# Seven block products for the first share of four more batches, and attention placed beside the other four

## The chip, the cores and the metric

One core of a Trainium2 chip runs the whole kernel. The metric is the device time of one execution in microseconds, the median of several runs. The five engines of the core that appear below are TensorE (PE, with its weight loads shown apart as PEld), VectorE (DVE), ScalarE (ACT), GpSimd (POOL) and SyncE (SP), whose queue issues all the DMAs of this kernel.

## The reference

Eight batches of eight heads, 512 local and 32 global positions, head size 64. Windowed attention feeds a gated feed-forward layer:

```python
k_all = np.concatenate([k_g, k_l], axis=2); v_all = ...
out_g = sm(scale * q_g @ k_all.T) @ v_all            # 32 global rows see everything
mask  = |i - j| <= 32                                # local rows: a band, and the 32 global keys
out_l = sm(concat([scale * q_l @ k_g.T, where(mask, scale * q_l @ k_l.T, -1e9)])) @ v_all
x = concat([out_g, out_l]).transpose(0, 2, 1, 3).reshape(4352, 512)
h = x @ w_in                                         # first product, w_in 512 x 2048
g = h * erf(softplus(h))
out = g @ w_out                                      # second product, w_out 2048 x 512
```

The inputs and weights are float32 and float64 respectively when they arrive; every large product is made of three float32r matmuls (high by high, high by low, low by high).

## The kernel before

**Two shares.** The 2048 hidden columns are 8 units of 256. Units 0 to 2 (`FIRSTU = 3`) are the first share, units 3 to 7 the second (`NQ = 5`). For each batch the first share computes h for 6 blocks of 128 columns, gates them (`gate`), multiplies them with their rows of w_out (`project`) and stores the sum to DRAM (`part`). The second share does the same for its units, loads the stored partial sum and adds it on the way out. The weights of the first share stay in SBUF (`W["in", 0, u]`). Those of the second share are split into parts early, kept in DRAM (`keep_in`, `keep_unit`) and read back later (`sums`, `fetch_unit`). The 32 global rows of all batches together make a ninth, smaller chunk, `c == B`.

**Two ways to do the first product.** In the first share, `unit` does it plainly: 4 blocks of the inner dimension by 3 matmuls, 12 matmuls of 128x512 for 128 columns of one batch. In the second share, `products` does it for two batches (`c = 2 * pr + j`) and one unit of 256 columns at once: a 2x2 by 2x2 block product by seven block multiplications instead of eight. Each of the seven (`product`) is 6 matmuls of 128x512, so a unit and a pair of batches take 42 matmuls where the plain way takes 48. For that, `pair_blocks` loads the pair's x, forms four sums on DVE and splits seven blocks into high and low; `keep_in` forms the sums on the side of the weights (`A11`, `A12`, `S1`, `A22`, `S2`, `S3`, `S4`); and the results are put together by two copies out of PSUM (`move`) and five additions on DVE (`fold`). The plain way has four copies out of PSUM for the same columns.

**Attention.** `attention` does a head: scores on PE, a masked maximum on DVE, a subtraction, the exponential on ACT, transposes on PE, the values on PE, and the normalisation mostly on DVE. The results go to DRAM (`xsc`, `xsg`) and are read back as x. The SBUF of attention is given to a second pool (`wb_pool`) once the last head is done (`ATTN`); the blocks that `pair_blocks` makes, the weight sums that `sums` loads, and part of the second share's w_out live there.

**What sets the order.** All work is entered as operations with a key, a list of engines that could do it, and an estimated duration. A planner (`Program.schedule`) walks through simulated time and gives each free engine the ready operation with the lowest key, so the instruction order on each engine is fixed when the kernel is built. Operations that may go to DVE or ACT go to whichever the planner expects free. POOL is offered to an operation that DVE can do only while the key lies under `SHARED[1]`. Keys count blocks of 128 columns of a batch: batch c of the first share has keys from 6c. Attention's heads have keys by `HKEYS`: before, head 64 lies at 33.2, so the attention is spread beside batches 0 to 5 and the PE work of the first share is mixed between its pieces.

**Order of the stages before.** Attention mixed with the first share of batches 0 to 6, then the global chunk, then batch 7 of the first share; then the second share by pairs 0 to 3; then the global chunk's second share. The lines: `keep_in` from 898, `unit` from 985, `gate` from 1021, `project` from 1074, `pair_blocks` from 1177, `products` from 1234, the loops from 1342. All matmuls are recorded at line 379, all DVE and POOL operations at 391, activations at 381, DMAs at 383.

Of the kernel before, what the change touches and what calls it, by code (L numbers as in the profile page):

```python
# [12 lines left out]
F32 = mybir.dt.float32  # L13
# [16 lines left out]
CROWD, STRETCH, EVADE = 254, 4.013, 0.302  # L30
# [5 lines left out]
HKEYS = ((0, -4.808), (11, -0.938), (22, 0.485), (64, 33.202))  # L36
STEP, GKEY = 0.082, -0.59
QLEAD, VLEAD, RLEAD, XLEAD = 0.802, -1.384, -3.274, 5.136
GOFF, POFF = 6.111, 3.439
WIN, WOUT = (1.692, -0.833, -2.539), (5.372, 5.751, 6.572)  # L40
BIASED, AG = 28, 3
SHARED = (-99.0, 10.395)
TPAIR = 3.723
KEEP, KSTEP, FIRST = 25.717, 1.786, (18.732, 17.811)
CVO = (54.239, 54.957, 78.914, 61.099, 65.318)
QLEAD2, XDEL, SLOTS = 2.849, -2.014, 11
GATE1, GATE2, PROJ1, PROJ2 = (18.529, 22.625, 24.302), (22.055, 24.328, 43.477), 16.064, 32.464
SPT = 0.35
BIAS, AHEAD = 1.579, 13.005
# [7 lines left out]
NEAR = 7.126  # L57
PAIRED, GOJOIN, GSJOIN, PTS = 16, 6, 5, 4
# [8 lines left out]
WLEAD = 2.131  # L67
LATER, GFIRST = 8, (-3.104, -5.093)
HOFF = (-0.552, -0.319, 0.052, -0.145, -0.077, -0.13, 0.035, -0.016, -0.005, -0.046, 0.01, -0.049, -0.013, 1.49, 2.105, -0.254, 0.767, 0.207, -0.21, 0.858, 0.388, -0.382, 1.584, -2.479, 0.129, -0.149, -0.895, 0.741, 3.078, -0.931, 2.609, 4.711)
XOFF = (-1.743, 3.531, 4.132, 6.479, -2.355, 1.289, 6.274, -1.424, -2.0)  # L70
UOFF = (2.693, -0.229, -0.111, -0.488, 10.393, -2.037, 0.678, -8.495, 2.152)
GFF = (-0.013, 0.75, -1.267, 1.697, -1.821, -1.427, -1.715, -1.652, -1.918)
PFF = (0.156, 0.123, 0.319, 0.471, 0.761, 2.958, 1.452, 0.32, -1.362)
KQ = (2.677, 1.804, -0.704, -0.365, 4.117, -1.317, 9.687, 0.998, 2.585, -6.754)
NORMAL = 1.125 * 2.0**-15
STRAIGHT, XLATE = True, -4.089
# [264 lines left out]
def kernel(  # L341
# [553 lines left out]
    wq = [dram.tile([P, 7, 2, 256], F32, name=f"wq{q}") for q in range(NQ)]  # L895
    WQ = {(q, m): fixed(None) for q in range(NQ) for m in range(7)}

    def keep_in(q, key):
        T = []
        for i in range(2):  # L900
            TOP = View(mbuf([P, 512], F32, f"top_l_in_{q}_{i}", ("wt", "wr")[i], 1))
            ABS = View(mbuf([P, 512], F32, f"abs_l_in_{q}_{i}", "os", 4))
            to_fp32(key + KSTEP * i, w_in[NU + q, i], f"l_in_{q}_{i}", TOP, ABS, (), 1.0)
            T.append(TOP)
# [31 lines left out]

        k = key + KSTEP
        part_of(A11, a11, k)
        part_of(A12, a12, k)
        part_of(A22, a22, k)  # L940
# [80 lines left out]
    def gate(ps, c, us, key, after=(), turn=(), line=()):  # L1021
# [13 lines left out]
        add(  # L1035
            {"ACT": 2.6 + 1.31 * (ps == 0) + 1.11 * len(us)},
# [37 lines left out]
    def project(ps, c, G, at, order, after=None):  # L1074
# [15 lines left out]
        for t in range(nt):  # L1090
            for n, rows in enumerate(order):
# [3 lines left out]
                    at(n) + 0.01 * t + (TPAIR * (t // 2) if ps == 0 else 0.0),  # L1095
# [5 lines left out]
            k = at(len(order) - 1) + 0.01 * t + (TPAIR * (t // 2) if ps == 0 else 0.0)  # L1101
# [10 lines left out]
            else:  # L1112
                load(k - NU + 2, O, part[c][P * t : P * t + P, :], 262, [PART[c, t]])
                last = c == B - 1 and t == nt - 1
# [31 lines left out]

    for u in range(NQ):
        keep_in(u, KEEP + 4 * KSTEP * u + KQ[u])
        keep_unit(u, KEEP + 4 * KSTEP * u + 2 * KSTEP + KQ[NQ + u])

# [9 lines left out]
    def sums(name, q, key, order):  # L1160

        M = {}
        for n, m in enumerate(order):
# [5 lines left out]
                [WQ[q, m], ATTN],  # L1169
# [7 lines left out]
    def pair_blocks(pr, key):  # L1177
# [3 lines left out]
        for n, (i, j) in enumerate(((0, 0), (0, 1), (1, 1), (1, 0))):  # L1181
            c = 2 * pr + j
            R[i, j] = mbuf([P, 2, SL], F32, f"rx_1_{c}_{i}", "raw", RAWS)
            src = xsc[c][2 * P * i : 2 * P * i + 2 * P, :].rearrange("(k p) t -> p k t", p=P)
            load(key + 0.05 * n, R[i, j], src, 1050, [XSC[c, p] for p in range(2 * i, 2 * i + 2)] + AFTER.get(pr, []))
        T = mbuf([P, 2, SL], F32, f"rt_{pr}", "raw", RAWS)
        blocks = {}

        def block(name, n, A, k):
            HL = [Buf(pool, [P, 2, SL], F32R, f"x{x}_{pr}_{name}", tag) for x, (pool, tag) in zip("hl", XTAG[2 * n : 2 * n + 2])]  # L1190
# [43 lines left out]
    def products(name, q, X, key):  # L1234
# [22 lines left out]
        PAIR = mbuf([P, 2, SL], F32R, f"pair_{name}", ("xh", "xl")[q % 2], 3)  # L1257
# [59 lines left out]
    def last_unit(q, X, key):  # L1317


        M = sums(f"g{q}", q, key - QLEAD2, (A11, A12, S1, A22))  # L1320
# [21 lines left out]
    s = -NV  # L1342
    for c in [*range(B - 1), B, B - 1]:
        s += NU if c == B - 1 else NV
# [4 lines left out]
        for a in range(0, n, AG):  # L1349
            G |= gate(0, c, us[a : a + AG], s + a + AG + GOFF + GFF[c])  # L1350
        key = s + AG + POFF + PFF[c]
        if c < B:
            project(0, c, G, lambda n: key + 2 * n, [[(2 * u + a, 0, 2 * u + a) for a in range(2)] for u in range(NU)])
        else:
            project(0, c, G, lambda n: key + n, [[(u, 256 * a, 2 * u + a) for a in range(2)] for u in range(NU)])
# [4 lines left out]

    s0 = 17 * NU
    turns, ACTS = (), fixed(None)
    AFTER = {}
    order = [[(v, 0, v) for v in (2 * u, 2 * u + 1)] for u in range(NQ)]
    for pr in range(B // 2):
        s = s0 + 4 * NQ * pr
        X = pair_blocks(pr, s - XDEL)
        one, two = [], []
        for q in range(NQ):
            a, b, more = products(f"{pr}_{q}", q, X, s + 4 * q)  # L1370
            one += [(2 * q, a[0], ()), (2 * q + 1, a[1], ())]
# [92 lines left out]
```

## Time and profile before

| | before |
|---|---|
| runs (3) | 904.61, 904.69, 908.22 us; median 904.69 |
| profiled execution | 904.46 us |
| its span, first to last instruction | 902.7 us |
| mean granted TensorE clock | 0.996 |
| busy share of the span | PE 98%, PEld 80%, DVE 76%, ACT 60%, POOL 1% |
| moved by DMA | 188.22 MB |

The busy share of PE counts pipelined matmuls that overlap, so a full row does not by itself say that the matmuls follow at their closest pace; the spacing of matmuls in the chain of waits says that. In the views by stage, the stages are: up to 90 us attention with little else; 90 to 388 us attention with the first share; 388 to 444 us the end of the first share; then four pairs of the second share, and from 860 us the last projections.

### The profile page before, as it was taken

What the parts mean: (1) busy time and instruction counts of PE and PEld (TensorE: products, weight loads), DVE (VectorE), ACT (ScalarE), POOL (GpSimd) and SP (SyncE); (2) the same over time, 40 slices, a digit from 0 to 9 for tenths busy, and PEclk for the clock granted to TensorE, in tenths of its full rate; (3) what the DMA queues carried; (4) which work ended last, traced back from release to release, by engine and by line L of the source; (5) the groups of instructions that cost most, each with busy time, mean ns of one, the idle gap of its engine ahead of it and who ended that gap; (6) DMA issues with size and microseconds to landing.
All of it is one profiled execution on the core that took longest, in us unless ns stands there. A gap on an engine that the chain in (4) does not pass through costs nothing.

```text
span 902.7 us, 22276 instructions
## 1 busy us (share of the span) xinstructions
PE 885.5 (98%) x8807; PEld 721.2 (80%) x8807; DVE 682.9 (76%) x1821; ACT 543.7 (60%) x912; POOL 12.1 (1%) x13
## 2 busy tenths in 40 slices
PE   8789999999999999999999999999999999999998
PEld 5567787888878888888888888888888888888886
DVE  6798999969997899987898686487736965465553
ACT  5667977736673796657645583565517571553850
POOL 0002100000000000000000000000000000000000
PEclk9899999999999999999999999999999999999999
DMA  9878886888769958377499836644366426436013
GB/s 337 305 231 286 263 266 211 242 269 278 241 217 299 318 177 292 125 273 274 168 297 369 278 95 192 225 117 129 110 171 211 150 86 195 139 108 213 19 48 117
DMA packets 110016, 188.22 MB, mean 209 GB/s; under 512 B 15576, under 2 KB 39384, under 8 KB 109912
## 3 DMA queue, kind: packets, MB, share of 16 engines
q1 hardware_dynamic: 109912, 186.79, 63.7%
q8 instruction: 70, 1.15, 0.5%
q14 instruction: 34, 0.28, 0.1%
HBM read 145.59 MB, written 41.16 MB: 207 GB/s over the span
## 4 chain that ended last, share of the span: by engine, by line
PE 89%; DMA 5%; DVE 2%; ACT 2%; issue 1%; SPq 1%; DVEq 0%; ACTq 0%
PE op L379 40%; PE h L379 13%; PE pd L379 6%; PE pc L379 6%; PE pa L379 6%; PE o L379 3%; PE pb L379 3%; PE s L379 3%; PE t L380 3%; PE h_g L379 2%; PE ga L379 1%; DMA vb<-in_vB_dram 1%; PE go L379 1%; SPq L383 1%; PE gt L380 1%
## 5 line engine op out<-in xcount | busy, mean ns | idle before, releaser
L379 PE MATMUL op<-wouth,gh 128*128 128x512 f32 x544 | 215.8, 397 | 0.0
L379 PE MATMUL op<-wouth,gl 128*128 128x512 f32 x544 | 212.1, 390 | 0.0
L379 PE MATMUL op<-woutl,gh 128*128 128x512 f32 x544 | 212.0, 390 | 0.0
L382 ACT ACT_TABLE_LOAD x108 | 138.6, 1283 | 2.6 <-PEq L1451 0.7
L379 PEld LDWEIGHTS op<-wouth,gl 128*128 128x128 f32 x544 | 102.1, 188 | 21.8
L379 PEld LDWEIGHTS op<-wouth,gh 128*128 128x128 f32 x544 | 102.2, 188 | 21.5 <-issue 0.6
L379 PEld LDWEIGHTS op<-woutl,gh 128*128 128x128 f32 x544 | 102.3, 188 | 19.5
L381 ACT ACTIVATE gh<-sp 128x512 fp32r<-128x512 f32 x65 | 40.2, 629 | 104.9 <-PE op L379 88.8
L391 DVE TENSOR_TENSOR gl<-sp,gh 128x512 fp32r<-128x512 f32 x134 | 90.4, 689 | 12.8 <-PE op L379 9.3
L379 PE MATMUL h<-xh,winh 128*128 128x512 f32 (+1 forms) x216 | 85.2, 395 | 0.0
L379 PE MATMUL h<-xh,winl 128*128 128x512 f32 (+1 forms) x216 | 81.9, 379 | 0.0
L379 PE MATMUL h<-xl,winh 128*128 128x512 f32 (+1 forms) x216 | 81.7, 378 | 0.0
L381 ACT ACTIVATE sp<-sp 128x512 f32<-128x512 f32 x136 | 75.9, 622 | 0.5
L391 DVE CUSTOM_DVE_ANT_0 sm<-s,cs 128x128 f32<-128x128 f32 x256 | 57.6, 285 | 15.4 <-PE s L379 8.3
L391 DVE CAST gh<-sp 128x512 fp32r<-128x512 f32 x71 | 29.2, 422 | 36.0 <-PE op L379 35.8
L379 PE MATMUL pd<-xh_T,wq 128*128 128x512 f32 x160 | 55.6, 389 | 0.0
L379 PE MATMUL pa<-xh_B,wq 128*128 128x512 f32 x160 | 55.6, 389 | 0.0
L379 PEld LDWEIGHTS h<-xh,winh 128*128 128x128 f32 x216 | 40.6, 188 | 9.8 <-issue 2.2
L379 PEld LDWEIGHTS h<-xh,winl 128*128 128x128 f32 x216 | 40.6, 188 | 8.0
L391 DVE TENSOR_TENSOR pair<-u,pc 128x512 f32<-128x512 f32 x40 | 27.4, 685 | 24.8 <-PE pc L379 24.5
L379 PEld LDWEIGHTS h<-xl,winh 128*128 128x128 f32 x216 | 40.7, 189 | 6.7
L379 PE MATMUL o<-vb,pt 128*32 128x65 f32 x1280 | 37.7, 221 | 7.0 <-issue 5.1
(160 smaller groups left out, 1640.3 us busy)
## 6 DMA issues: line engine op xcount, KB each, us to landing
wq<-wq SPq DMA_DIRECT2D x140, 256.0 KB, 3.0
vb<-in_vB_dram SPq DMA_DIRECT2D x64, 325.0 KB, 5.6
rx<-xsc SPq DMA_DIRECT2D x30, 512.0 KB, 5.5
va<-in_vA_dram SPq DMA_DIRECT2D x64, 195.0 KB, 5.4
k<-in_kE_dram SPq DMA_DIRECT2D x32, 384.0 KB, 5.0
wq<-part SPq DMA_DIRECT2D x35, 256.0 KB, 5.0
q<-in_qT_dram SPq DMA_DIRECT2D x32, 272.0 KB, 4.5
part<-os SPq DMA_DIRECT2D x34, 256.0 KB, 4.6
```

Source lines behind the costliest of these rows:

```text
L379: pe = lambda n, *a, **k: pinned(nc.tensor.matmul(n, *a, **k))
L380: tr = lambda *a, **k: pinned(nc.tensor.transpose(*a, **k))
L381: act = lambda *a, **k: pinned(nc.scalar.activation(*a, **k))
L382: table = lambda name: pinned(nc.scalar.preload_act_table_set(name))
L383: dma = lambda *a, **k: pinned(nc.sync.dma_start(*a, **k))
L391: return lambda *a, **k: pinned(f(*a, **k))
```

## The change

A constant `NS = 2` says how many pairs of batches take the seven block products in the first share as well. Batches 4 to 7 are pairs 2 and 3. `REG = B - 2 * NS` batches (0 to 3) keep the plain way. The order becomes: attention mixed with the first share of batches 0 to 3, the global chunk, pairs 2 and 3 of the first share by `products`, then the second share with pair 3 first (it uses again the blocks of x that the first share left in SBUF) and pairs 0 to 2 after it. `keep_in` now also runs for units 0 to 2: it adds the resident high and low parts back together, copies three of the seven weight parts to DRAM by DMA out of SBUF as they are, and forms the four others. The constants of the planner are new throughout: attention's last key is 20.24 in place of 33.2, and the global rows' scores and values are no longer put into one operation with a head's (`GOJOIN`, `GSJOIN` 8, which no batch reaches; before 6 and 5). `gate` returns to the table of the exponential only for batches that still have attention beside them.

```diff
-HKEYS = ((0, -4.808), (11, -0.938), (22, 0.485), (64, 33.202))
+HKEYS = ((0, -4.601), (11, -1.503), (22, 0.501), (64, 20.24))
...
-SHARED = (-99.0, 10.395)
+SHARED = (-99.0, 7.131)
...
-KEEP, KSTEP, FIRST = 25.717, 1.786, (18.732, 17.811)
+KEEP, KSTEP, FIRST = 24.238, 1.426, (1.496, 21.886)
...
-NEAR = 7.126
-PAIRED, GOJOIN, GSJOIN, PTS = 16, 6, 5, 4
+NEAR = 17.282
+PAIRED, GOJOIN, GSJOIN, PTS = 16, 8, 8, 4
...
+NS = 2
+KIN = (11.987, 14.584, 17.071)
+GA1, GA2, PA1, PA2 = (1.46, 8.335, 10.948), (11.676, 20.938), 6.21, 10.581
...
     def keep_in(q, key):
         T = []
+        resident = W["in", 0, q] if q < NU else None
         for i in range(2):
+            if resident:
+                TOP = View(mbuf([P, 512], F32, f"top_l_in_{q}_{i}", ("wt", "wr")[i], 1))
+                add(
+                    {"DVE": 0.6, "POOL": 1.27},
+                    key + KSTEP * i,
+                    lambda e, i=i, TOP=TOP: vec[e].tensor_tensor(
+                        TOP.ap(), resident[0].ap[:, i, :].bitcast(F32), resident[1].ap[:, i, :].bitcast(F32), ALU.add
+                    ),
...
+        def copy_of(m, i, r, k):
+            WQ[q, m] = [fixed(None) for _ in range(2)]
+            for x, t in enumerate(resident):
+                src = lambda t=t: t.ap[:, i, :].bitcast(F32).rearrange("p (k r c) -> p k r c", k=2, r=2)[:, :, r]
+                dst = wq[q][:, m, x].rearrange("p (k c) -> p k c", k=2)
+                add({"SP": SPT}, k, lambda src=src, dst=dst: dma(dst, src()), [t], [WQ[q, m][x]], moved=131.0)
...
-            if ps == 0:
+            if back:
                 table(SET_EXP)
...
+    for u in range(NU if NS else 0):
+        keep_in(u, KIN[u])
...
-    s = -NV
-    for c in [*range(B - 1), B, B - 1]:
-        s += NU if c == B - 1 else NV
+    REG = B - 2 * NS
+    PO = [*range(B // 2 - (NS > 0), B // 2), *range(B // 2 - (NS > 0))]
+    LASTC = 2 * PO[-1] + 1
+    for n, c in enumerate([*range(REG), B]):
+        s = NV * n
         n = NV if c < B else NU
...
+    s1 = NV * REG + NU
+    for i, pr in enumerate(range(B // 2 - NS, B // 2)):
+        s = s1 + 4 * NU * i + AOFF[i]
+        X = pair_blocks(pr, s - XDELA[i], "0")
+        share(0, s, pr, [*range(NU)], [(2 * i, 2 * i + 2, k) for i, k in enumerate(GA1)], [(0, 4, GA2[0]), (4, 6, GA2[1])], PA1, PA2, X, None)
+    s0 = s1 + 4 * NU * NS
+    before = None
+    for i, pr in enumerate(PO):
+        s = s0 + 4 * NQ * i
+        if i or not NS:
+            X = pair_blocks(pr, s - XDEL)
...
+        share(1, s, pr, [NU + q for q in range(NQ)], first, [(0, 4, g[0]), (4, 8, g[1]), (8, 10, g[2])], PROJ1, PROJ2, X, before)
+        before = 2 * pr + 1
```

`share` is the body of the old loop over pairs: `products` for each unit, `gate` for the groups of blocks, `project` for the two batches.

## Rows read from the trace of the kernel before

**Rows 1.** Windows by stage: us of PE, PEld, DVE, ACT, POOL; clock, DMA share, GB/s.
```profile
0.00:90.00 90.00, 77.86 (x1803) 55.73 (x1803) 72.28 (x310) 59.66 (x150) 9.59 (x11) 0.96 0.85 290
90.00:180.00 90.00, 88.58 (x1694) 70.65 (x1696) 82.50 (x319) 71.18 (x137) 2.53 (x2) 1.00 0.78 244
180.00:388.00 208.00, 208.00 (x2975) 168.26 (x2966) 184.60 (x618) 132.61 (x217) 0.00 (x0) 1.00 0.77 248
388.00:444.00 56.00, 56.00 (x283) 47.76 (x282) 45.31 (x87) 39.92 (x60) 0.00 (x0) 1.00 0.65 235
444.00:546.00 102.00, 102.00 (x452) 84.46 (x451) 85.64 (x147) 63.45 (x97) 0.00 (x0) 1.00 0.74 250
```
**Rows 2.** Chain of waits in order of time: start us, us, what.
```profile
303.50 2.95 PE h L379 x12
...
412.61 16.32 PE h L379 x72
...
443.89 1.36 PE pa L379 x6
```
**Rows 3.** Windows of the first product's plain matmuls, tile h, two stretches.
```profile
90.00:180.00 90.00, 29.96 (x120) 22.00 (x120) 2.06 (x3) 4.95 (x9) 1.00 0.78 244
180.00:388.00 208.00, 79.56 (x324) 59.53 (x324) 2.73 (x4) 13.74 (x23) 1.00 0.77 248
```
**Rows 4.** Windows of the projections, tile op, the same two stretches.
```profile
90.00:180.00 90.00, 22.28 (x84) 14.92 (x84) 1.28 (x2) 1.18 (x2) 1.00 0.78 244
180.00:388.00 208.00, 78.29 (x309) 56.11 (x310) 3.33 (x5) 6.49 (x11) 1.00 0.77 248
```
**Rows 5.** Windows of attention's scores (tile s), then of its values (tile o).
```profile
90.00:180.00 90.00, 10.69 (x576) 8.12 (x576) 15.87 (x71) 1.00 0.78 244
180.00:388.00 208.00, 13.87 (x768) 10.66 (x768) 23.42 (x104) 1.00 0.77 248
...
90.00:180.00 90.00, 10.13 (x544) 8.34 (x542) 9.06 (x35) 0.93 (x4) 1.00 0.78 244
180.00:388.00 208.00, 16.69 (x960) 14.30 (x960) 15.59 (x59) 0.93 (x4) 1.00 0.77 248
```
**Rows 6.** Groups by line: the scores of all 64 heads.
```profile
L379 PE MATMUL s<-k,q 64*32 64x128 f32 x2048 | 37.8, 274 | 3.0 <-DVE mx L391 1.5 <-issue 0.6 <-DMA k<-in_kE_dram 0.5
```
**Rows 7.** Who waited for whom, PE from 90 to 388 us, the longest wait.
```profile
PE gx L379 <- DVE xg L391: 0.5, 1, 0.5
```
**Rows 8.** Windows of keep_in (tile top_l_in), then keep_unit (tile top_k_out): DVE and ACT.
```profile
180.00:388.00 208.00, 33.13 (x74) 3.77 (x9) 1.00 0.77 248
...
180.00:388.00 208.00, 16.54 (x27) 1.90 (x3) 1.00 0.77 248
```
**Rows 9.** Groups by line on DVE: count | busy us, mean ns | idle before.
```profile
L391 DVE TENSOR_TENSOR pair<-u,pc 128x512 f32<-128x512 f32 x40 | 27.4, 685 | 24.8 <-PE pc L379 24.5
L391 DVE TENSOR_TENSOR rx<-rx,rx 128x1024 f32<-128x1024 f32 x4 | 4.9, 1223 | 0.1
L391 DVE TENSOR_TENSOR xl_B<-rx,xh_B 128x512 fp32r<-128x512 f32 x24 | 15.5, 687 | 0.0
L391 DVE TENSOR_TENSOR top_l_in<-top_l_in,top_l_in 128x256 f32<-128x256 f32 x15 | 6.3, 420 | 0.1
L391 DVE CAST part<-top_l_in 128x256 fp32r<-128x256 f32 x18 | 5.0, 284 | 2.1 <-DMA wq<-part 2.1
L391 DVE TENSOR_TENSOR xl<-rx,xh 128x512 fp32r<-128x512 f32 (+1 forms) x32 | 21.0, 699 | 0.0
L391 DVE CAST xh<-rx 128x512 fp32r<-128x512 f32 (+1 forms) x28 | 10.0, 402 | 3.7 <-PE h L379 2.5 <-DMA rx<-xsc 1.2
L391 DVE CAST gh<-sp 128x512 fp32r<-128x512 f32 x71 | 29.2, 422 | 36.0 <-PE op L379 35.8
```
**Rows 10.** Groups by line on ACT, columns as in rows 9.
```profile
L381 ACT ACTIVATE gh<-sp 128x512 fp32r<-128x512 f32 x65 | 40.2, 629 | 104.9 <-PE op L379 88.8
L382 ACT ACT_TABLE_LOAD x108 | 138.6, 1283 | 2.6 <-PEq L1451 0.7
```

More of the change, by code (lines that the diff above doesn't have):

```diff
@@ L1019, in unit, with gate @@
         return v, Hb, ()
-    def gate(ps, c, us, key, after=(), turn=(), line=()):
+    def gate(ps, c, us, key, after=(), turn=(), line=(), back=False):
         SP = [mbuf([P, SL], F32, f"sp_{ps}_{c}_{v}", "sp", 6) for v, _, _ in us]
@@ L1031, in erf @@
                 act(SPb.ap, SPb.ap, AF.Erf)
-            if ps == 0:
+            if back:
                 table(SET_EXP)
         add(
-            {"ACT": 2.6 + 1.31 * (ps == 0) + 1.11 * len(us)},
+            {"ACT": 2.6 + 1.31 * back + 1.11 * len(us)},
             key,
@@ L1113, in project @@
                 load(k - NU + 2, O, part[c][P * t : P * t + P, :], 262, [PART[c, t]])
-                last = c == B - 1 and t == nt - 1
+                last = c == LASTC and t == nt - 1
                 for i in range(2 if last else 1):
@@ L1349 @@
         for a in range(0, n, AG):
-            G |= gate(0, c, us[a : a + AG], s + a + AG + GOFF + GFF[c])
+            G |= gate(0, c, us[a : a + AG], s + a + AG + GOFF + GFF[c], back=c < B)
         key = s + AG + POFF + PFF[c]
         if c < B:
-            project(0, c, G, lambda n: key + 2 * n, [[(2 * u + a, 0, 2 * u + a) for a in range(2)] for u in range(NU)])
+            project(0, c, G, lambda n: key + 2 * n, [[(2 * u + a, 0, 2 * u + a) for a in range(2)] for u in range(NU)], halves=True)
@@ L1354, with share @@
         else:
-            project(0, c, G, lambda n: key + n, [[(u, 256 * a, 2 * u + a) for a in range(2)] for u in range(NU)])
+            project(0, c, G, lambda n: key + n, [[(u, 256 * a, 2 * u + a) for a in range(2)] for u in range(NU)], halves=True)
     for u in range(NQ):
         fetch_unit(u, CVO[u])
-    s0 = 17 * NU
     turns, ACTS = (), fixed(None)
     AFTER = {}
[L1364 to L1367, printed above, removed]
+    def share(ps, s, pr, units, groups1, groups2, at1, at2, X, before):
+        nonlocal turns
@@ L1368 @@
         one, two = [], []
-        for q in range(NQ):
-            a, b, more = products(f"{pr}_{q}", q, X, s + 4 * q)
-            one += [(2 * q, a[0], ()), (2 * q + 1, a[1], ())]
-            two += [(2 * q, b[0], (more,)), (2 * q + 1, b[1], (more,))]
-        for us, c, g, at in ((one, 2 * pr, GATE1, PROJ1), (two, 2 * pr + 1, GATE2, PROJ2)):
+        for n, u in enumerate(units):
+            a, b, more = products(f"{ps}_{pr}_{u}", u, n, X, s + 4 * n)
+            v = 2 * (u - units[0])
+            one += [(v, a[0], ()), (v + 1, a[1], ())]
+            two += [(v, b[0], (more,)), (v + 1, b[1], (more,))]
@@ L1374 @@
+        order = [[(v, 0, v) for v in (2 * n, 2 * n + 1)] for n in range(len(units))]
+        for us, c, groups, at in ((one, 2 * pr, groups1, at1), (two, 2 * pr + 1, groups2, at2)):
             G = {}
-            for a, z, k in ((0, 2, FIRST[0]), (2, 4, FIRST[1]), (4, 8, g[1]), (8, 10, g[2])) if c == 0 else ((0, 4, g[0]), (4, 8, g[1]), (8, 10, g[2])):
+            for a, z, k in groups:
                 turn = fixed(None)
-                G |= gate(1, c, us[a:z], s + k, turns, [turn], [ACTS])
+                G |= gate(ps, c, us[a:z], s + k, turns, [turn], [ACTS])
@@ L1380 @@
     s = s0 + 4 * NQ * (B // 2)
-    X = last_blocks(s - XLEAD)
-    us = [last_unit(q, X, s + q) for q in range(NQ)]
+    X = last_blocks(s - XLEAD + LOFF[0])
+    us = [last_unit(q, X, s + q + LOFF[1]) for q in range(NQ)]
     G = {}
```

94 lines of the change are left out of this document (56 added, 38 removed).

## The prediction

> **What bounds the kernel now.** I read the windows by stage first, then the chain of waits, then the counts of PE's work in two stretches, and last the groups by line, for prices. From 180 to 546 us PE has no idle time in any stage, at the full granted clock of 1.00 (2.4 GHz), and ScalarE and GpSimd have plenty [rows 1]. A busy PE row counts overlapping matmuls, so the pace has to be taken from the chain: the plain h matmuls of batch 7 stand in one piece, 72 in 16.32 us, and six matmuls of a block product take 1.36 us [rows 2]. Both are 0.2267 us a matmul, with nothing that they wait for. So behind the attention PE alone sets the time, and a matmul removed there gives its 0.2267 us back.
>
> Inside the attention the reader should check whether that still holds. From 90 to 180 us 120 matmuls of h and 84 of op ran [rows 3, 4], 204 x 0.2267 = 46.2 us; the other 43.8 us of PE belong to attention. A head has 2048 / 64 = 32 score instructions [rows 6], and as many for the values by the code, so 576 and 544 [rows 5] are 18 and 17 heads, 17.5 in the mean: 2.50 us a head. From 180 to 388 us it is 633 x 0.2267 = 143.5 us of large matmuls, 64.5 us for 24 and 30 heads, in the mean 27: 2.39 us a head. The two prices are close, though a head has 204 / 17.5 = 11.7 large matmuls beside it in the first stretch and 23.4 in the second, and the longest time PE waited for anyone in both is 0.5 us [rows 7]. So PE sets the pace there too, but with VectorE close behind: 82.50 of 90 us (92%) and 184.60 of 208 us (89%) [rows 1].
>
> **The change part by part.** The time is summed against the profiled execution: 904.46 us, of which 902.7 are span; that is 0.2 under the median of the runs, 904.69.
>
> *Matmuls removed.* Two pairs by three units by (48 - 42) matmuls are 36 matmuls, 36 x 0.2267 = 8.16 us. The projections, 72 matmuls a batch, stay. Nothing else of PE changes in number but fillers.
>
> The Trainium skill, page "TensorE: Matmul & The Clock Gate", section "Back-to-back issue gap", gives a sustained 131 ns for a 512-column matmul in a stream with its weight loads; by it the 36 would be worth 4.7 us. The trace disagrees: 227 ns in an unbroken stretch of 72 [rows 2].
>
> *Attention against fewer batches.* By 388 us PE had done about 504 matmuls of h (60 before 90 us) and 393 of op; now it has 288 and 288 at most beside the heads. The heads that ran at 11.7 large matmuls each cost 2.50 us, and the new mixture has about that ratio: at most (516 matmuls left after 90 us) / 44.5 heads = 11.6. If the thin mixture is what costs 0.11 us a head, 27 heads more cost 3.0 us. On the other side, a piece of 12 h matmuls between attention pieces takes 2.95 us in the chain against 12 x 0.2267 = 2.72 [rows 2], 0.23 us for going back and forth. Up to 20 h pieces and 35 op pieces leave the mixture; if fewer than half of them now pay that, up to 5 us come back. I take 0 between -5 and +3, since the two stretches and the pieces point opposite ways.
>
> *VectorE.* Added: five folds for each of six products, 30 x 0.685 = 20.6 us; weight sums of three resident units, 6 additions x 0.685 + 12 x 0.420 + 12 low parts x 0.420 + about 6 casts x 0.284 = 15.9; one more set of blocks, since five are built and not four (pair 3's are used twice), 4 x 1.223 + 14 x 0.687 + about 5 casts x 0.422 = 16.6. Removed: the plain x of four batches, 16 x 0.699 + 14 x 0.402 = 16.8 [rows 9]. Twelve copies out of PSUM go as well; I leave them at nothing, as they are split with ACT. Net 36.3 us.
>
> Where that falls matters more than the sum. Before, 33.1 + 16.5 = 49.7 us of keeping the second share's weights lay between 180 and 388 us [rows 8]. With attention squeezed, most of it has to go behind, beside the pairs' first share and the first pair of the second share, because that pair uses all five units. So take the stretch from 90 us to the end of that first pair: VectorE was busy 82.50 + 184.60 + 45.31 + 85.64 = 398.1 of 456 us, 87% [rows 1]. After, the same content is 398.1 + 36.3 = 434.3 us, in 456 - 8.2 = 447.8 us, 97%. That would be tight. What relieves it: ACT was idle 18.8 + 75.4 + 16.1 + 38.6 = 149 us in the same stretch [rows 1], and casts and PSUM copies may go to either engine. A cast taken by ACT frees 0.422 us and costs 0.629 [rows 9, 10], so 24 us off VectorE cost ACT about 36 of its 149 idle us. At the 92% that VectorE kept from 90 to 180 us without holding PE up, 434.3 - 24 fit into 447.8 us exactly. Bounds: if ACT takes nothing, 434.3 / 0.917 = 473.6 us, a stall of 25.8; if it takes 24 or more, none. I take 1.7, a relief of about 22 us.
>
> *ACT.* Batches 4 to 7 of the first share had 4 x 2 x 3 = 24 table loads; the two pairs have 2 x 5 x 2 = 20. Four fewer, 5.1 us at 1.283 [rows 10], on an engine that isn't the bound: nothing.
>
> *DMAs, all on SP's queue.* Six products read 42 weight sums of 256 KB, 10.5 MB in the 122 us of the pairs' first share (540 matmuls), about 86 GB/s, and the three resident units write 5 MB. From 388 to 546 us the engines were busy 0.65 and 0.74 of the time at 235 and 250 GB/s, with 290 GB/s and 0.85 seen at the start [rows 1]. Room is there; the cover is that each sum is loaded several products ahead. I count nothing; without the cover, each product waits for a transfer of some us, and the bound is that of the slower rival.
>
> *The hand-over.* The blocks' SBUF comes free only with the last head, and three blocks wait for the resident weights too. The work that hides it: the projections of batches 2 and 3, keyed behind head 64, at 72 matmuls x 0.2267 = 16.3 us a batch. Without it, a load, sums and casts of some 10 us lie bare. Nothing counted.
>
> Sum: 904.5 - 8.2 + 0 + 1.7 + 0 = 898.0 us.
>
> **The rivals.**
> - *VectorE becomes the bound (slower).* One mechanism: the keeping of the weights is pushed behind the attention, ACT takes too little, and the products of the pairs' first share and of the first second-share pair wait for blocks and weight parts. It decides by the relief: with x us taken off VectorE the stretch takes (434.3 - x) / 0.917. Below x = 12 the kernel is over 909; x = 10 gives 462.7, a stall of 14.9, 911 us; x = 0 gives 922. For it: 97%. Against: windows of 92% with no PE wait longer than 0.5 us [rows 1, 7], and ACT's 149 us. The Trainium skill, page "Perfetto Trace Analysis", section "Identifying the Most-Contended Engine", calls PE's matmul busy share misleading and takes the weight loads' share; by that, from 90 to 388 us PE stands at 80% under VectorE's 90%, and VectorE is the engine to spare, which speaks against this change. The trace bears it out only as a ranking. Chance 0.16.
> - *The gain goes into the attention (no change).* Thin cover at 2.50 us a head: 904.5 - 8.2 + 1.7 + 3.0 = 901.0; or the relief lies between 12 and 20 us, 900 to 909. For it: heads are dearer where there is less beside them. Against: 0.11 us is the difference of two rough counts, and the exposed pieces argue the other way. Chance 0.22.
> - *The matmuls are worth less than their spacing.* 36 matmuls at 0.131 us give 904.5 - 4.7 + 1.7 = 901.5. Against it stands the spacing in the chain [rows 2]. Chance 0.02. The 131 ns are those of the Trainium skill's page "TensorE: Matmul & The Clock Gate" above.
>
> **How the numbers follow.** The forecast, PE bound throughout with most of 8.2 us kept, has 0.60, and 893 to 900 as its own range. The low end is 904.5 - 8.2 - 5 = 891, the attention pieces' bound; the high end is 911, the slower rival at x = 10. Beyond them I leave about 0.04 below and 0.12 above. A measurement of this kernel tells 0.5%, 4.5 us, from no change: under 900.2 is faster, over 909.2 slower. Faster 0.60; same 0.22 + 0.02 = 0.24; slower 0.16.
>
> **What would show it right or wrong.** Right: 36 fewer large matmuls, pieces of six at 1.36 us in the pairs' first share; the last head near 90 + 44.5 x 2.45 + at most 117 us, so 280 to 316 us; PE without idle time behind it; VectorE near 719 us in all and at 90 to 95% from 90 us to the end of the first second-share pair, with more casts on ACT. Wrong: PE waits of several us on weight parts, blocks or sums between the attention's end and the second pair (the slower rival); a head's price clearly over 2.5 us (the second); or a clock under 1.00 where PE starves. A DMA share near 1.0 with products waiting for weight sums would be an error in the transfer step.

## The result and the profile after

The changed kernel takes 912.46 us (median of 7 runs, 909.30 to 915.88) against 905.08 us for the kernel before beside it: a ratio of 1.0078, 95% interval 1.0057 to 1.0100. It is slower by over 0.5%, and 912.46 lies above the range of 891 to 911. The profiled execution took 913.88 us, 912.1 of it span, so the span grew by 9.4 us where the forecast had it fall by 6.5.

The windows by stage, cut where the attention's last values end (310.75 us; the kernel before started its last ones at 372.5). Columns: us of PE, PEld, DVE, ACT, POOL; clock, DMA share, GB/s:

```profile
0.00:90.00 90.00, 74.82 (x1894) 53.85 (x1902) 74.22 (x348) 62.06 (x168) 8.99 (x11) 1.00 0.93 315
90.00:310.75 220.75, 210.85 (x4160) 166.45 (x4158) 201.82 (x788) 145.91 (x252) 0.00 (x0) 1.00 0.89 282
310.75:912.10 601.35, 593.98 (x2706) 494.50 (x2706) 437.25 (x763) 321.83 (x471) 0.00 (x0) 1.00 0.57 186
```

In [rows 1] PE had no idle time from 180 us on. Here it has 9.9 us of it beside the attention, and the DMA engines, at 0.77 to 0.78 there before, stand at 0.89; VectorE is at 91%. The same stage in the windows of the first product (h) and of the projections (op), PE first:

```profile
90.00:310.75 220.75, 63.95 (x252) 45.54 (x252) 5.46 (x8) 7.76 (x13) 1.00 0.89 282
...
90.00:310.75 220.75, 55.75 (x211) 37.38 (x211) 2.02 (x3) 4.19 (x7) 1.00 0.89 282
```

With 36 matmuls of h before 90 us that makes 288 + 211 = 499 large matmuls up to the end of the attention, as the prediction had it (288 and 288 at most). Taken off at 0.2267 us each, they leave 310.75 - 113.1 = 197.6 us for everything else of that stage. Before, up to 388 us, it was 388 - (504 + 393) x 0.2267 = 184.7 us. So the same 64 heads cost 13.0 us more, 3.09 us each and not 2.89. A later execution of the same kernel (h0_after_again, below) has a span of 906.1 us and starts its last values at 304.7: 305.0 - 113.1 = 191.9, so 7.2 us more. The two executions differ by 6.0 us in span and by 5.8 us in the end of the attention: this kernel's spread is made there.

PE's idle time tells the same. Up to the end of the attention it is 15.2 + 9.9 = 25.1 us here and 13.7 + 6.9 = 20.7 us in the later execution, whose rows these are; before, it was 12.1 + 1.4 = 13.6 us [rows 1]. That is 11.5 of the 13.0 us, and 7.1 of the 7.2.

```profile
0.00:90.00 90.00, 76.27 (x1931) 55.49 (x1940) 74.92 (x349) 63.34 (x171) 9.00 (x11) 0.98 0.95 320
90.00:305.00 215.00, 208.07 (x4138) 165.16 (x4122) 201.34 (x787) 145.27 (x249) 0.00 (x0) 1.00 0.90 288
```

The chain of waits shows what took PE's place (start us, us, what; SPq is SP's queue):

```profile
134.30 0.60 DVE top_l_in L398
...
137.69 0.62 DVE xT L398
138.31 0.57 DVE pt L398
138.88 0.34 DVE top_l_in L398
139.30 6.02 DMA xsc<-xT
145.34 0.42 SPq L390
...
146.84 0.48 SPq L390
147.42 5.42 DMA va<-in_vA_dram
...
154.00 2.95 PE h L386 x12
156.95 1.09 PE o L386 x64
158.06 3.67 DMA va<-in_vA_dram
...
166.52 0.40 SPq L390
166.96 3.16 DMA vb<-in_vB_dram
...
190.77 6.61 DMA wq<-part
```

It should be read as links of one chain: VectorE's keeping of weights (top_l_in) and its part of the attention, a store of transposed x to DRAM that waits for that, SP's queue behind the store, and then the values (va, vb) that a head needs and that come late. The chain says what to test, and not yet what holds the stage: of PE's idle time up to the end of the attention, its list of waits puts only 3.6 us down to values (the lines stand at a3 below). In the kernel before, the chain runs from 137 us on nearly without a break over PE, pieces like those of [rows 2]. The windows of 30 us, with the scores (tile s) under them, give the pace:

```profile
150.00:180.00 30.00, 29.58 (x561) 22.72 (x559) 28.93 (x115) 19.38 (x34) 0.00 (x0) 1.00 0.86 260
...
210.00:240.00 30.00, 28.17 (x585) 21.30 (x575) 27.29 (x108) 16.81 (x29) 0.00 (x0) 1.00 0.95 304
...
150.00:180.00 30.00, 3.84 (x192) 2.78 (x192) 5.36 (x24) 1.00 0.86 260
...
210.00:240.00 30.00, 3.47 (x192) 2.67 (x192) 5.35 (x24) 1.00 0.95 304
```

Each window holds 192 scores, six heads, 5.0 us a head, with VectorE at 96% in one and the DMA engines at 0.95 in the other.

Behind the attention PE is dense, as forecast. Its chain and the longest wait there (us in total, times, longest):

```profile
337.60 1.36 PE pa L386 x6
338.96 1.36 PE pc L386 x6
340.32 1.36 PE pd L386 x6
...
359.36 8.16 PE op L386 x36
```

```profile
PEld pc L386 <- DVE pair L398: 0.6, 1, 0.6
```

What did change there is the end. The stores of the result issued behind 895 us, first of the kernel before and then of the kernel after (count, KB each, median us from issue to landing):

```profile
out_dram<-os SPq DMA_DIRECT2D x3, 256.0 KB, 2.0
out_dram<-os SPq DMA_DIRECT2D x2, 128.0 KB, 1.8
```

```profile
out_dram<-os SPq DMA_DIRECT2D x4, 256.0 KB, 6.3
out_dram<-os SPq DMA_DIRECT2D x2, 128.0 KB, 5.2
```

Not every landing is in the trace: in the kernel after, the medians are those of the last two stores of 256 KB and of both of 128 KB. The last VectorE work ends at 899.90 us before, 2.8 us ahead of the span's end, and at 905.69 after, 6.4 us ahead: 3.6 us more in which nothing but stores runs. So the 9.4 us are -8.2 for the matmuls, +13.0 in the attention, +3.6 at the end, and about 1 for the rest. In the execution with a span of 906.1 they are -8.2 + 7.2 + 3.6 and 0.8 for the rest, 3.4 in all.

### The profile page after: what moved, and what is told of

The parts are those of the page before. It is cut to its first block, busy times and chain, and to the rows that moved or that the text cites. A ratio compares the mean times of both kernels' runs of the same rounds, so it can differ in the third digit from the quotient of the medians.

```text
span 912.1 us, 22364 instructions
## 1 busy us (share of the span) xinstructions
PE 879.7 (96%) x8757; PEld 714.8 (78%) x8764; DVE 713.3 (78%) x1897; ACT 529.8 (58%) x889; POOL 9.0 (1%) x11
## 2 busy tenths in 40 slices
DMA packets 121600, 202.63 MB, mean 222 GB/s; under 512 B 16664, under 2 KB 45080, under 8 KB 121496
## 4 chain that ended last, share of the span: by engine, by line
PE 79%; DVE 8%; DMA 7%; issue 2%; ACT 2%; SPq 1%; DVEq 0%
PE op L386 38%; PE pc L386 7%; PE pd L386 7%; PE pa L386 7%; PE h L386 5%; PE pb L386 4%; DVE sm L398 2%; DMA va<-in_vA_dram 2%; PE s L386 2%; PE o L386 2%; DMA vb<-in_vB_dram 2%; PE h_g L386 2%; PE t L387 1%; SPq L390 1%; PE ga L386 1%
## 5 line engine op out<-in xcount | busy, mean ns | idle before, releaser
L386 PE MATMUL pd<-xh_ih_T,wq 128*128 128x512 f32 x208 | 72.1, 390 | 0.0
L386 PE MATMUL pa<-xh_x_B,wq 128*128 128x512 f32 x208 | 71.7, 389 | 0.0
L398 DVE CUSTOM_DVE_ANT_0 sm<-s,cs 128x128 f32<-128x128 f32 x256 | 57.1, 286 | 11.4 <-PE s L386 11.4
L388 ACT ACTIVATE u<-pa 128x512 f32<-128x512 f32 x18 | 10.7, 596 | 65.0 <-PE pa L386 64.9
L386 PE MATMUL h<-xh,winh 128*128 128x512 f32 (+1 forms) x120 | 47.4, 395 | 0.0
L386 PEld LDWEIGHTS pd<-xh_ih_T,wq 128*128 128x128 f32 x208 | 39.0, 188 | 8.4 <-DVE u L398 0.3
L386 PE MATMUL s<-k,q 64*32 64x128 f32 x2048 | 40.5, 274 | 5.1 <-issue 1.9
L386 PEld LDWEIGHTS pa<-xh_x_B,wq 128*128 128x128 f32 x208 | 39.0, 188 | 8.1
L386 PE MATMUL h<-xl,winh 128*128 128x512 f32 (+1 forms) x120 | 44.4, 370 | 0.0
L386 PE MATMUL h<-xh,winl 128*128 128x512 f32 (+1 forms) x120 | 44.4, 370 | 0.0
L388 ACT ACTIVATE sm<-sm,mx 128x128 f32<-128x128 f32 x112 | 35.1, 394 | 14.8 <-DVE mx L398 14.7
```

The source lines that it names most:

```text
L386: pe = lambda n, *a, **k: pinned(nc.tensor.matmul(n, *a, **k))
L388: act = lambda *a, **k: pinned(nc.scalar.activation(*a, **k))
L398: return lambda *a, **k: pinned(f(*a, **k))
```

## The experiments

Theory C ("cover"): PE still sets the pace in the attention, and a head costs it more where it has fewer large matmuls beside it. Theory S ("supply"): a head needs so much of VectorE and of the transfers that, with fewer matmuls beside it, these set the pace, and PE waits. A third question is the end: late stores or not. All runs keep the order of instructions that the kernel's planner gives; only the edit shown differs. Ratios are against the kernel before run beside each; the last column is the start of the last value matmul in the profiled execution.

| run | made from | median us | ratio [95%] | last values |
|---|---|---|---|---|
| kernel before | | 905.08 | | 372.5 |
| kernel after | | 912.46 | 1.0078 [1.0057, 1.0100] | 310.5 |
| h0_after_again | after | 910.09 | 1.0053 [1.0036, 1.0071] | 304.7 |
| a1_third_out | after | 906.25 | 1.0006 [0.9980, 1.0032] | 303.4 |
| f2_no_subtract | after | 909.32 | 1.0044 [1.0021, 1.0067] | 305.6 |
| f1_half_values | after | 904.38 | 0.9980 [0.9957, 1.0003] | 299.7 |
| f1c_small_values | after | 905.03 | 1.0006 [0.9983, 1.0029] | 301.4 |
| f12_both | after | 899.54 | 0.9929 [0.9905, 0.9954] | 296.0 |
| f12b_before_both | before | 902.86 | 0.9956 [0.9942, 0.9970] | 372.8 |
| a2_store_pool | after | 909.41 | 1.0037 [1.0017, 1.0058] | 303.6 |
| a3_values_pool | after | 915.19 | 1.0102 [1.0058, 1.0146] | 311.1 |
| p2_before_thin | before | 893.70 | 0.9866 [0.9823, 0.9909] | 369.6 |
| f4_no_weight_sums | after | 908.21 | 1.0025 [1.0004, 1.0045] | 302.9 |
| g0_split_global | after | 905.39 | 1.0006 [0.9985, 1.0027] | 307.3 |
| g1_all_kept | after | 902.12 | 0.9959 [0.9945, 0.9974] | 304.3 |
| g2_before_same | before | 905.70 | 1.0001 [0.9982, 1.0019] | 373.5 |
| h1_reliefs_split | after | 896.56 | 0.9901 [0.9878, 0.9924] | 296.7 |

The unchanged kernel after came out at 1.0078 and at 1.0053, so a single edit counts only where its interval is clear of both.

**Does PE set the pace beside the heads? (a1_third_out).** One of the three terms of the plain matmuls of batches 0 to 3 is left out, 192 matmuls, 192 x 0.2267 = 43.5 us.

```diff
-                pe(o, wl, xh, start=False, stop=(k == NKT - 1))
+                if c >= 4:
+                    pe(o, wl, xh, start=False, stop=(k == NKT - 1))
...
-                pe(OP[t].ap, lh, WL.ap[:, v % 2, :], start=False, stop=False)
+                if ps or c >= 4:
+                    pe(OP[t].ap, lh, WL.ap[:, v % 2, :], start=False, stop=False)
```

> The changed kernel, same order of instructions, but the plain matmuls of batches 0 to 3 in the first share leave out their third term (low weights by high x in the first product, high by low weights in the projection): 192 matmuls, 43.5 us at 0.2267, some 166 of them (38 us) beside the attention. Theory C (PE still sets the pace in the attention and a head only costs it more): about 869 us. Theory S (what feeds PE there, VectorE or SP's queue with its transfers, sets the pace once the cover is thin): PE waits instead, only the 6 us behind the attention and a little more come off: 890 to 906 us.

Of 43.5 us, 4 to 7 came off the median, and 26 of the matmuls left out, 5.9 us, stand behind the attention. The last values start at 303.4 us, where the unchanged kernel has 304.7 and 310.5. Under C the attention should have ended up to 38 us earlier (166 matmuls beside it). From 90 to 300 us PE is now idle for 28 us and VectorE and the DMA engines are as full as before:

```profile
90.00:300.00 210.00, 182.07 (x3941) 139.37 (x3940) 198.71 (x784) 142.71 (x248) 0.00 (x0) 0.98 0.93 293
```

So C falls for the kernel after, and S stands. What follows is which part of the supply.

**VectorE alone (f2_no_subtract).** In the 36 heads in which VectorE subtracts the maximum ahead of the exponential, the subtraction is left out (the softmax is the same function); 36 x 0.687 = 24.7 us less on VectorE.

```diff
-                lambda e: vec[e].tensor_tensor(
-                    SM.ap, SM.ap, MX.ap.unsqueeze(2).to_broadcast([P, 4, P]), ALU.subtract
-                ),
+                lambda e: None,
```

> The changed kernel, same order, but heads 28 to 63 leave out the subtraction of the row maximum on VectorE (the softmax is the same without it): 36 operations of 0.685 us, 24.7 us off VectorE, nothing off the transfers. Theory S with VectorE as the one that binds: the attention ends 10 to 16 us earlier, 896 to 902 us. Theory S with SP's queue and its transfers: within 3 us of the changed kernel, 909 to 915. Theory C: the same.

VectorE's busy time from 90 to 300 us fell to 178.6 us of 210 (85%), and the time is not told from that of the kernel after (1.0044). VectorE alone is not what holds it.

```profile
90.00:300.00 210.00, 202.17 (x4073) 161.89 (x4072) 178.56 (x740) 140.69 (x247) 0.00 (x0) 1.00 0.92 291
```

**Transfers alone (f1_half_values, f1c_small_values).** Odd heads of batches 2 to 7 load no values and use those of the head ahead of them: 48 loads and 12.8 MB less (189.84 MB in all, and not 202.63). In the second kernel these 48 loads are issued, but move 64 bytes a partition.

```diff
+        def value(n, dst, src):
+            if b < 2 or h % 2 == 0:
+                dma(dst.ap, src)
+            else:
+                dst.ap = V0[n].ap
```

> The changed kernel, same order, but the odd heads of batches 2 to 7 load no values and use those of the head before: 48 DMAs and 12.5 MB less on SP's queue, nothing off VectorE. Theory S with SP's queue and its transfers as what binds: the attention ends 10 to 16 us earlier, 896 to 902 us. Theory S with VectorE: within 3 us, 909 to 915. Theory C: the same.

> The changed kernel, same order; the odd heads of batches 2 to 7 still issue their two value loads, but of 64 bytes a partition, and use the values of the head before: the issues stay, 12 MB of bytes go. If the bytes in flight are what the half value loads took away: 903 to 906 us, as there. If it is the issue time and the place in SP's queue: 909 to 913.

0.9980 and 1.0006: both clear of 1.0053 and 1.0078. The first, at 904.38 us, lies between its two expectations. With 12.8 MB less the attention ends 5 to 11 us earlier; with the issues kept and the bytes gone, 3 to 9. So it is mostly the bytes. In the first, VectorE now stands at 96% of the stage, next in line:

```profile
90.00:300.00 210.00, 206.96 (x4160) 165.29 (x4159) 201.26 (x789) 146.00 (x252) 0.00 (x0) 1.00 0.79 238
```

**Both, and the control on the kernel before (f12_both, f12b_before_both).** The two edits above together.

> The changed kernel, same order, with both reliefs: heads 28 to 63 without the subtraction on VectorE and odd heads of batches 2 to 7 without value loads. If VectorE and the transfers bind at different places by turns (after leaving out one, 1 and 0.3% came back), the gains add up: 898 to 901 us, ratio about 0.993. If both reliefs shorten the same wait: 903 to 905, ratio about 0.998.

> The control: the kernel before, same order, with the same two reliefs (heads 28 to 63 without the subtraction on VectorE, odd heads of batches 2 to 7 without value loads). If PE sets the pace in the kernel before and VectorE and the transfers only in the changed one: within 3 us of the kernel before, ratio over 0.997. If the kernel before is held by the same supply: as much as in the changed kernel, some 13 us, ratio about 0.986.

The kernel after comes to 0.9929, some 11 to 13 us less than without; the kernel before gains 4 us, and its last values start where they did (372.8 against 372.5). After has PE full again:

```profile
90.00:300.00 210.00, 209.49 (x4180) 168.87 (x4179) 188.02 (x767) 147.51 (x257) 0.00 (x0) 1.00 0.79 242
```

The last values start at 296.0 us; 296.3 - 113.1 = 183.2 us for all but the large matmuls, against 184.7 before. With supply to spare a head costs PE what it cost before. Thin cover is no price of its own: it lays bare the supply. The control gains a little more than the 3 us that its first expectation allowed. Where the 4 us came from wasn't found: its attention is no shorter, and its profiled execution, with a span of 902.9 us, does not show them.

**The place in SP's queue (a2_store_pool, a3_values_pool).** The chain passes through SP's queue. In one kernel the 112 stores of transposed x are issued from GpSimd's queue, in the other the 128 loads of values.

```diff
-                        dma(rows[a], XT.ap[WB * a : WB * a + WB])
+                        pinned(nc.gpsimd.dma_start(rows[a], XT.ap[WB * a : WB * a + WB]))
...
-        load(key - VLEAD, VA, vA[b, h], 200)
-        load(key - VLEAD, VB, vB[b, h], 333)
+        far = lambda d, s: pinned(nc.gpsimd.dma_start(d.ap, s))
+        add({"SP": SPT}, key - VLEAD, lambda: far(VA, vA[b, h]), [], [VA], moved=200)
+        add({"SP": SPT}, key - VLEAD, lambda: far(VB, vB[b, h]), [], [VB], moved=333)
```

> The changed kernel, same order, but the 112 small stores of attention's result (64 KB each) are issued from GpSimd's queue and not from SP's; the bytes stay. If it is the place in SP's queue and the time to issue that binds: 897 to 906 us. If it is the bytes in flight: 910 to 914. If it is VectorE: 910 to 914.

> The changed kernel, same order, but the 128 value loads are issued from GpSimd's queue and not from SP's, bytes unchanged, so that they no longer stand behind stores that wait for VectorE. If place and issue time in SP's queue bind: 898 to 905 us. If bytes in flight: 908 to 913. A slower way of making descriptors on GpSimd would show as longer landing times and could cost more than 913.

1.0037, not told from 1.0053, and 1.0102. In the second kernel (a3) PE hardly waited for values any more, and the attention was no shorter. PE's waits for values up to the end of the attention, first in the kernel after, then in a3 (us in total, times, longest):

```profile
PE o L386 <- DMA vb<-in_vB_dram: 2.1, 4, 1.0
...
PE go L386 <- DMA va<-in_vA_dram: 1.5, 1, 1.5
```

```profile
PE o L386 <- DMA vb<-in_vB_dram: 0.5, 1, 0.5
```

And what GpSimd's queue waited for in a3 from 90 to 310 us, before it issued a load of values:

```profile
POOL va L471 <- PE o L386: 90.8, 16, 9.4
POOL va L471 <- PE go L386: 72.2, 8, 12.4
```

For 163 of 220 us that queue stood ready and waited until PE had done with a buffer of values, so the loads went out as early as their buffers allow, and the last values still start at 311.1 us. So neither the order in SP's queue nor late values are the cause by themselves; the chain's last link is a sign of the supply and not what sets its pace. The test isn't a clean one: the loads of 325 KB took a median of 6.3 us to land there and not 5.1, PE was busy for 3.3 us less in the first 90 us, and 13.5 us of its waits (11.4 in the kernel after) name nothing that ended them.

**Was the kernel before bound by PE there? (p2_before_thin).** In the kernel before, the plain matmuls of the first share of all eight batches keep one of their three terms: 768 matmuls, 174 us, are left out. By 372.7 us it ran 282 large matmuls against 834, so 552 x 0.2267 = 125 us of PE's work are gone from beside the heads.

> The kernel before, same order, but the plain matmuls of the first share for all eight batches leave out their second and third term: 768 matmuls, 174 us, of which 598 (136 us) stood beside the attention. This is the kernel before with thin cover and none of the new work. If PE sets the attention's pace: the last head's values at about 240 us, 731 us in all. If the attention has a floor of its own of about 5 us a head, set by VectorE and the transfers: its last values between 295 and 315 us, 780 to 800 us in all.

Both expectations missed, by 90 us and more. The last values start at 369.6 us and not at 372.5; only the work behind the attention got shorter. Windows of the thinned kernel, and two of its waits from 90 to 440 us:

```profile
0.00:370.00 370.00, 280.11 (x5812) 202.62 (x5823) 323.19 (x1209) 254.38 (x492) 12.31 (x13) 0.89 0.80 261
...
180.00:300.00 120.00, 87.86 (x1698) 65.31 (x1698) 101.46 (x370) 66.03 (x116) 0.00 (x0) 0.87 0.83 268
300.00:388.00 88.00, 62.75 (x896) 46.33 (x880) 85.86 (x256) 71.54 (x110) 0.00 (x0) 0.83 0.70 231
```

```profile
PEld h L379 <- DVE hs L391: 11.9, 4, 4.2
...
PEld o L379 <- DMA vb<-in_vB_dram: 9.8, 7, 5.4
```

PE was idle for a quarter of the stage and the heads still came only 3 us sooner. So in this order of instructions something other than PE holds the attention of the kernel before as well. How near the two are can't be read from this run, for where PE idled the granted clock fell to 0.83 to 0.87. Of the 122 us that did not come off, 76 are more idle time of PE (89.9 us up to 370 us, where the full kernel has 13.6 up to the same point of the attention); the other 46, an estimate, went into a slower PE. At the full clock the heads might have come earlier than 369.6 us.

**The keeping of weight sums (f4_no_weight_sums).** Units 0 to 2 make no weight sums (additions, low parts and 12 stores are left out, and the products read one stored part for them).

> The changed kernel, same order, but units 0 to 2 leave out the weight sums and their parts: the six additions, the twelve sums, the parts and their 12 stores of 256 KB (15.9 us of VectorE and ACT work by the prediction, 3.1 MB); the products read the block A11 in place of the four sums. The 18 copies of resident parts stay. If this added work in the squeezed attention makes most of the loss: 902 to 905 us. If the loss is mainly the attention's old work meeting less cover: 908 to 911.

1.0025, between the two expectations, and not clear of 1.0053. If it is a gain, it is under 5 us: a share of the load, not the cause.

**The end (g0_split_global).** Two 256 KB stores, those of the global rows, each go to four places of 32 rows in DRAM. In the kernel before they were issued at 880.8 and 882.3 us, 13 us ahead of the last five stores; after, at 900.2 and 901.6 us, with the last four behind them within 4.2 us. Here each is issued as four DMAs of 32 rows.

```diff
-                        lambda t=t, O=O, cols=cols: dma(out_rows(c, t)[..., cols], O.ap[:, cols]),
+                        lambda t=t, O=O, cols=cols: [
+                            dma(out[(4 * t + n) * SQ : (4 * t + n) * SQ + SG, cols], O.ap[SG * n : SG * n + SG, cols])
+                            for n in range(4)
+                        ]
+                        if c == B
+                        else dma(out_rows(c, t)[..., cols], O.ap[:, cols]),
```

> The changed kernel, same order; each of the two last stores of the global rows (four blocks of 32 rows in one DMA) is issued as four DMAs of 32 rows. Theory: these two stand between the last ordinary stores now and land slowly (up to 6.7 us), so the span ends 6.4 us after the last work where it was 2.8. If the form of that DMA is what is slow: the end comes 3 to 4 us earlier, ratio about 1.004 to before. If it is the bytes of six stores at once: within 1 us of the changed kernel, ratio about 1.007.

The stores issued behind 895 us:

```profile
out_dram<-os SPq DMA_DIRECT2D x8, 64.0 KB, 1.7
out_dram<-os SPq DMA_DIRECT2D x2, 256.0 KB, 2.2
out_dram<-os SPq DMA_DIRECT2D x2, 128.0 KB, 1.8
```

The last work ends at 902.82 us and the span at 905.7: 2.9 us, as in the kernel before, and 3.5 less than in the kernel after. Not only the split stores but the ordinary ones beside them land as fast as before (1.8 and not 5.2 us). The median is at 1.0006, which is more than 3.5 us under the kernel after; the attention of this execution ended 3 us earlier by itself, within that kernel's spread. The Trainium skill, page "DMA: Bandwidth & Descriptors", section "Why a DMA increments its semaphore by 16 and not by 1", says that a transfer runs on the largest number of engines up to 16 that divides the slowest dimension of both its sides; for four blocks that would be four. The trace agrees. In the kernel after, the DMA share stands at 0.26 right behind these two stores, four engines of 16, and the two ordinary 256 KB stores issued behind them take 6.3 us in the median; the 6.7 us of the expectation are the slower of these ordinary two, and not a time of the stores in four blocks, whose landing the trace lacks. The DMAs of 32 rows take 1.7 us.

```profile
901.80:904.50 2.70, 2.70 (x13) 2.24 (x12) 1.38 (x2) 0.00 (x0) 0.00 (x0) 1.00 0.26 48
...
out_dram<-os SPq DMA_DIRECT2D x2, 256.0 KB, 6.3
```

**A version that keeps the result (g1_all_kept, g2_before_same).** The edits of f2, a2 and g0 together leave the result as it is. On the kernel after and, as a control, on the kernel before:

> The changed kernel, same order, with three edits that leave the result what it was: global stores in four DMAs, attention's small stores from GpSimd's queue, no subtraction of the maximum for heads 28 to 63. If the parts add up as the two reliefs did (0.3 + 0.4 + 0.4%): ratio about 0.997, 902 us, as fast as the kernel before or a little faster. If the stores and the subtraction shorten the same waits: 905 to 906.

> The control: the kernel before, same order, with the same three edits. If PE sets its pace: within 2 us of the kernel before, ratio over 0.998. If it is as near its supply as the changed kernel: 899 to 901, ratio about 0.994, and the change brings nothing even with them.

0.9959 [0.9945, 0.9974] and 1.0001 [0.9982, 1.0019]. With these edits the change is 0.4% faster than the kernel before with or without them, some 3 to 4 us. Its last values start at 304.3 us, where the unchanged kernel has 304.7 and 310.5, so of this gain the trace shows the end (3.3 us of stores alone, and not 6.4) and no shorter attention.

**All reliefs, and the kernel after once more (h1_reliefs_split, h0_after_again).** f1, f2 and g0 together; odd heads of batches 2 to 7 use the values of others, as in f1.

> The changed kernel, same order, with both reliefs (no subtraction for heads 28 to 63, no value loads for odd heads of batches 2 to 7) and the global stores in four DMAs. If the 36 matmuls are worth their 8.2 us once supply and end are as good as before: ratio 0.989, 895 to 896 us, 6 us under the kernel before with the same reliefs (0.9956). If something else still holds it: 0.992 to 0.993, as without the split stores.

> The changed kernel unchanged, timed once more beside the next one, because the attention of the run before ended 3 us earlier with nothing changed there, and the parts of 3 us found for single edits rest on this kernel's own time. If its time holds: ratio 1.006 to 1.010. If it came out slow the first time: 1.003 to 1.005, and the single parts of 0.3% are not told from it.

0.9901 [0.9878, 0.9924], with a mean granted clock of 1.00 and a span of 894.2 us, 8.5 under the kernel before. Against the kernel before with the reliefs of VectorE and the values (0.9956) it is 0.55%, about 5 us.

## Why the prediction was wrong

*The bound.* The step that failed is "So PE sets the pace there too, but with VectorE close behind". It rested on no idle time in [rows 1] and no wait over 0.5 us in [rows 7]. Both are true and neither shows that PE is the only bound: with 125 us of matmuls gone the heads of the kernel before came 3 us sooner (p2, where a lower clock took part of it), and with 38 us gone those of the kernel after came 1 us sooner than in its own better execution (a1). In that stage PE was covering a supply with little to spare. The rows that said so were read as room: VectorE at 89% and the DMA engines at 0.77 of [rows 1].

*Attention against fewer batches.* Taken at 0, between -5 and +3; it measured +13.0 and +7.2 in two executions. The two prices of a head, 2.50 and 2.39 us, were PE's prices, and they hold (183 us for the rest of the stage in f12, 184.7 before). What was not counted is what a head takes of the others. Beside the attention after, VectorE is busy 91% and the DMA engines 0.89 of the time; relieving VectorE alone was not told from nothing, relieving the transfers gave 0.7 to 1.0%, both gave 1.2 to 1.5%. The lower bound of -5 had a slip of its own: by the counts given, 18 pieces of h leave the mixture and not 20, and 105 matmuls of op in pieces of 6 or 12 are 18 pieces at most, not 35; half of these 36 pay 0.23 us each, 4 us.

*DMAs, "I count nothing".* This looked at the pairs' first share behind the attention, where it was right. The total grew from 188.2 to 202.6 MB. But beside the attention most of the traffic is not new: the heads' own loads fell into less time, at 282 GB/s from 90 to 310.75 us, where [rows 1] has 244 and 248. Leaving 3.1 MB of the new stores out (f4) was not told from the later execution. Nothing was counted for the hand-over either, and there that was right: PE's chain runs on without a gap.

*Matmuls removed, -8.16.* The pieces of six take 1.36 us in an unbroken chain, and with the supply and the end relieved (h1) the span is 894.2 us against 902.7, the size that the prediction had. Against the control with the same two reliefs about 5 us of it are seen; the rest lies within what f12b gained for a reason not found.

*VectorE, +1.7, and ACT, 0.* VectorE was forecast near 719 us and has 713.3; table loads were to be four fewer than 108 and are 103. Behind the attention PE's longest wait for VectorE is 0.6 us. The 1.7 us were near the truth by another way than the one counted. From 90 to 540 us, near the end of the first second-share pair, VectorE is busy 406 us (90%), where the sum had 434 less a relief of 22. But little of that is ACT's doing, which makes 56 casts of gh and made 65 [rows 10]; 20 us lie behind that pair instead (233 us there, and 212.6 before). And the keeping of weights did not go behind as a whole: top_l_in takes 36.15 us of VectorE beside the attention, where it took 33.13 [rows 8]; only top_k_out left. The three rows (the second: DVE, then ACT):

```profile
90.00:540.00 450.00, 439.94 (x5200) 356.77 (x5199) 406.10 (x1166) 286.68 (x461) 0.00 (x0) 1.00 0.83 273
...
90.00:310.75 220.75, 36.15 (x82) 3.73 (x9) 1.00 0.89 282
...
L388 ACT ACTIVATE gh<-sp 128x512 fp32r<-128x512 f32 x56 | 34.6, 627 | 67.0 <-PE op L386 44.2 <-DVE sp L398 22.7
```

So the rival "VectorE becomes the bound" had the right sign and a wrong place and mechanism: not products that wait for kept weights behind the attention, but heads that VectorE and the transfers together hold up inside it. The Trainium skill, page "Perfetto Trace Analysis", section "Identifying the Most-Contended Engine", ranks VectorE by its busy share, PE by that of its weight loads, and the DMA engines by HBM utilization; the prediction's rival compared the first two and left the third out. For the kernel after, a1 agrees that the stage was not PE's, and f1 shows the transfers to be the larger part. For the kernel before, sparing VectorE, which that comparison puts first, did not shorten the attention: its last values start at 372.8 us in f12b and 373.5 in g2, against 372.5.

*"The gain goes into the attention".* Right in its place, and too small: 3.0 us were counted, 0.11 us on each of 27 heads; 7 to 13 us came, 0.11 to 0.20 on each of all 64, and the matmuls' gain was eaten whole. Its reason was wrong too: PE was not dearer beside thin cover, it waited.

*The end.* Nothing in the prediction looked at which stores land last. 3.6 us of the loss are there.

Not shown is which transfers hold the heads: f1 takes 12.8 MB off the DMA engines, and all other transfers beside the heads gain by that; a3 says that it is not the lateness of the values alone. Not tried: a version with one pair in place of two, the kernel before with its attention moved ahead and nothing else changed, and a later keeping of the second share's weights. Whether a planner's order made for the supply could feed the attention at 296 us without leaving loads out stays open.

## What to carry to other kernels

A full engine without waits is the bound only if the others could go faster: before taking work away from beside a stage, work out what the shorter stage asks of its loads and of each other engine; here the attention, had it ended at some 297 us (310.75 less the 13.0), would have asked for the 74.2 + 201.8 us of VectorE that it used, 93% of the time, and for 90 x 315 + 220.75 x 282 GB/s, 90.6 MB, so 305 GB/s, which is nearly the 315 that the first 90 us reach at a DMA share of 0.93. A run that leaves the covering work out, like p2 or a1, tests it in one go, if the granted clock is read beside it. After a reordering, look at the last stores as well: which they are, and how long each takes to land.

## What the runs showed of the hardware

With PE idle for a quarter of the time in p2, the granted clock was 0.90, 0.87 and 0.83 in successive stretches from 90 to 388 us, where the full kernel has 1.00; work left out beside the attention came back in part as matmuls at the lower of its two levels (1.2 of 2.4 GHz). An ordinary 256 KB store of the result took 6.7 us to land behind two stores in four blocks; with those split, none of the last stores took over 2.3 us. The 128 KB stores beside them took 5.2 and 1.8 us. Behind the two stores in four blocks the DMA share was 0.26. Loads of values from GpSimd's queue (325 KB) took a median of 6.3 us to land from 90 to 310 us, 5.1 from SP's; PE's waits for values fell from 3.6 to 0.5 us, and the attention ended no earlier (last values at 311.1 us against 304.7 and 310.5).
